# Attention output and second-parity x turned in 32x32 blocks by VectorE and put together through a DRAM scratch

## The chip, the cores and the metric

The kernel runs on one core of one Trainium2 chip. A core has a matrix engine (TensorE, PE in the profile), a vector engine (VectorE, DVE), a scalar engine (ScalarE, ACT), GpSimd (POOL) and SyncE (SP), which here only issues transfers to the core's 16 DMA engines. Each engine runs its own instructions in the order of the program and waits on semaphores for the others. The metric is the device time of one execution in microseconds (us). Lower is better.

## The reference

```python
x = A_x                                    # 1 x 2048 x 576, float32
xn = _layernorm(x, axis=-1)                # (x - mean) / sqrt(var + 1e-5)
return x + _A_ref(xn, A_wqkv, A_wo) + _B_ref(xn, B_w1, B_w2)

# _A_ref: 32 heads of 18; each position attends to itself and 7 earlier ones, 2 apart
qkv = xn @ wqkv                            # 576 -> 3 x 576
logits = einsum("bhsd,bhswd->bhsw", q, kg) * 18 ** -0.5     # masked where idx < 0
o = einsum("bhsw,bhswd->bhsd", softmax(logits), vg)
return o @ wo                              # 576 -> 576

# _B_ref
return relu(xn @ w1) @ w2                  # 576 -> 4608 -> 576
```

All of it is float32. The kernel reaches that accuracy with matmuls of a rounded type (float32r): each operand is split into a rounded part and the rest, and the products that matter are added.

## The kernel before

**Tiles and phases.** The attention only joins positions of one parity, since it steps by 2. So the kernel runs two phases (`ph` 0 and 1), one for each parity, of 1024 positions: 8 tiles (`i`) of 128 rows by 576 columns, held in `X`. A tile must also be there turned (columns on the partitions) as the operand of matmuls. 576 columns are 4 full groups of 128 and one of 64; the fifth group holds the 64 twice, so that one of its halves can carry the rounded part and the other the rest. Two tiles make one `XT` block of 256 positions (4 blocks, `tb`), with 9 groups: 4 rounded, 1 mixed, 4 rests.

**The loop and its order.** A phase has 144 steps: 12 chunks of the 4608 hidden columns, in each chunk 4 blocks `tb`, in each 3 slices `f` of 128 columns. The loop at line 547 writes out each engine's program step by step. In a step `n` it gives out, in this order: `run_splits` (weights that came by DMA are split by ACT and VectorE, and further loads issued), `h_mm(n+2)` (14 matmuls, then ReLU on ACT at line 447 and the rest on VectorE at line 448), the `at` list of the step, `o_mm(n)` (12 matmuls; after the third slice VectorE adds to `X` at line 471), the `late` list of the step, and `run_bg` (attention work of VectorE, as much as the planner's account of time allows). There are two buffers for the result of `h_mm` (`ph`), and `o_mm` works on what `h_mm` gave two steps earlier. Within an engine nothing is reordered.

**Attention** is taken in 4 units of 8 heads: `qkv_tile` on TensorE, the products and sums on VectorE from the `bg` queue into `QO`.

**Output projection.** From step 123 of a phase on, `wo_a` (late list) turns tile `i` of `QO` by five TensorE transposes (`transpose_split`, lines 273 and 274) into PSUM, and ACT and VectorE split it into `oT`. In the next step `wo_b` (at list) multiplies by the split `wo` in 28 matmuls, VectorE adds the result to `X`, and `done` stores the tile once it has all its parts. One tile is taken each step.

**Second-parity x.** At the end of phase 0 (the last chunk starts at step `e` = 132) the x tiles of phase 1 are loaded, `stats` and `norm` make the normalized tile `xn`, and `make_xt` turns it by five TensorE transposes and splits it into `XT`. Tile `i` has its `z = e + 3 + 2i`: load at `z - 6`, statistics late at `z - 2`, norm late at `z - 1`, `make_xt` at `z + 1`. The first `h_mm` of phase 1 that needs the block of tiles 6 and 7 is that of step 151.

**Queues.** All loads and stores but the halo copies of k and v are issued by SP, in program order: weights (lines 157 to 162, 173, 190 to 193, 210 to 213), x (235), out (432). Weights are loaded three tasks ahead of their split.

Of the kernel before, what the change touches and what calls it, by code (L numbers as in the profile page):

```python
# [10 lines left out]
F32 = mybir.dt.float32  # L11
F32R = mybir.dt.float32r
AF = mybir.ActivationFunctionType
ALU = mybir.AluOpType
# [3 lines left out]
P = 128  # L18
# [9 lines left out]
EPS = 1e-5  # L28

UNIT0, UNIT_STEP, WO_AT = 7, 27, 8  # L30
HEADW = (-5, -2, -1, 0, 0, 1)

HEAD = (
# [22 lines left out]
def tile_body(ctx: ExitStack, tc: tile.TileContext, x, wqkv, wo, w1, w2, out):  # L56
    nc = tc.nc
    S, D = x.shape
# [5 lines left out]
    KT = 4  # L64
    DR = D - KT * P
    D2 = D // 2
# [4 lines left out]
    ctx.enter_context(tc.manual_schedule())  # L71
    pool = lambda name, bufs, **k: ctx.enter_context(tc.tile_pool(name=name, bufs=bufs, **k))
    consts = pool("consts", 1)
    xp = pool("xp", 12)
    xtp = pool("xtp", NTB)
    qop = pool("qop", 1)
    kp = pool("kp", 1)
# [7 lines left out]
    lgp = pool("lgp", 2)  # L85
    smp = pool("smp", 2)
    tmp = pool("tmp", 2)
    ps_o = pool("ps_o", 2, space=PSUM)
    ps_h = pool("ps_h", 2, space=PSUM)
    ps_m = pool("ps_m", 2, space=PSUM)  # L90

    f32 = lambda ap: ap.bitcast(F32)
# [18 lines left out]
    def mm(o, l, r, start, stop, n):  # L111
        nc.tensor.matmul(o, l, r, start=start, stop=stop)  # L112
        t["pe"] += n / 2400.0 + 0.002

    def dve(n):
        t["dve"] += (n + 130) / 960.0
# [109 lines left out]
            split_task(step, *one(kt))  # L226


    X, XT, XN, MR = {}, {}, {}, {}

    def load_x(ph, i, parts=1):
        X[ph, i] = xp.tile([P, D], F32, name="x")
# [18 lines left out]

    def norm(ph, i, act=False):
        nm, r = MR.pop((ph, i))
        xn = tmp.tile([P, 640], F32, name="xn")
        if act:
            nc.scalar.activation(xn[:, 0:D], X[ph, i], AF.Identity, bias=nm)  # L256
            nc.scalar.activation(xn[:, 0:D], xn[:, 0:D], AF.Copy, scale=r)  # L257
        else:
            nc.vector.tensor_scalar(xn[:, 0:D], X[ph, i], nm, r, op0=ALU.add, op1=ALU.mult)
            dve(600)  # L260
        nc.scalar.activation(xn[:, D:640], xn[:, KT * P : D], AF.Copy)
        XN[ph, i] = xn

    def transpose_split(src, last, hi, mix, lo, free=False):

        if free:
            pa, pb = (ps_o.tile([P, 2, 512], F32, name="po")[:, 0, :] for _ in range(2))
            pa, pb = pa.rearrange("p (k c) -> p k c", k=KT), pb[:, 0:P]
        else:
            pa = ps_m.tile([P, KT, P], F32, name="pm")  # L270
            pb = ps_m.tile([P, P], F32, name="pm")
        for k in range(KT):
            nc.tensor.transpose(pa[:, k, :], src[:, k * P : (k + 1) * P], ident)  # L273
        nc.tensor.transpose(pb, last, ident)  # L274
        t["pe"] += 5 * 0.06
        nc.scalar.activation(hi, pa, AF.Copy)  # L276
        nc.vector.tensor_tensor(lo, pa, f32(hi), op=ALU.subtract)
        nc.scalar.activation(mix, pb, AF.Copy)
        nc.vector.tensor_tensor(mix[DR:P], pb[DR:P], f32(mix[DR:P]), op=ALU.subtract)
        dve(512)  # L280
        dve(128)

    def make_xt(ph, i, free=False):
        tb, h = divmod(i, 2)
        if h == 0:
            XT[ph, tb] = xtp.tile([P, 9, TBN], F32R, name="xT")
        d = XT[ph, tb][:, :, h * P : (h + 1) * P]
        xn = XN.pop((ph, i))
        transpose_split(xn[:, 0:512], xn[:, 512:640], d[:, 0:4, :], d[:, 4, :], d[:, 5:9, :], free)


    TERMS = [(k, k) for k in range(KT)] + [(5 + k, k) for k in range(KT)] + [(4, 4)] + [(k, 5 + k) for k in range(5)]


    QO, KK, VV = {}, {}, {}
# [109 lines left out]
    OT = {}  # L405

    def wo_a(ph, i):
        assert (ph, i) in ready, (ph, i, len(bg))
        o = QO[ph][:, i, :]
        od = tmp.tile([P, 2, DR], F32, name="od")  # L410
        nc.scalar.activation(od, o[:, None, KT * P : D].to_broadcast([P, 2, DR]), AF.Copy)
        d = tmp.tile([P, 9, P], F32R, name="oT", bufs=1)
        transpose_split(o[:, 0:512], od.rearrange("p a b -> p (a b)"), d[:, 0:4, :], d[:, 4, :], d[:, 5:9, :])
        OT[ph, i] = d

    def wo_b(ph, i):
        d, w = OT.pop((ph, i)), WO[ph]
        po = [ps_m.tile([P, D2], F32, name="pm") for _ in range(2)]
        for j, (a, b) in enumerate(TERMS):
            for h in range(2):  # L420
                mm(po[h], d[:, a, :], w[b][:, h * D2 : (h + 1) * D2], j == 0, j == len(TERMS) - 1, D2)
        for h in range(2):
            acc = X[ph, i][:, h * D2 : (h + 1) * D2]
            nc.vector.tensor_tensor(acc, po[h], acc, op=ALU.add)
            dve(D2)
# [53 lines left out]
    def at(n, f, *a):  # L479
        todo.setdefault(n, []).append((f, a))  # L480
# [3 lines left out]
    def late(n, f, *a):  # L484
        todo_late.setdefault(n, []).append((f, a))

    plan = []
    for ph in range(NPH):
        b = ph * SPP
        for c in range(NCH):  # L490
            for f in range(C):
                s = b + c * SPC + f
                first = ph == c == 0
                plan.append((HEADW[f] if first else s - 5, w1_task, ((ph, c, f), c * C + f)))
                plan.append((HEADW[3 + f] if first else s - 3, w2_task, ((ph, c, f), c * C + f)))
        for u in range(NU):
            s = b + UNIT0 + u * UNIT_STEP
            plan.append((s - 5, wq_tasks, ((ph, u), u)))
            for i in range(NI):
                at(s + i, qkv_tile, ph, u, i)  # L500
            late(s + NI + 1, attention, ph, u)
        s = b + UNIT0 + NU * UNIT_STEP + WO_AT
        plan.append((s - 8, wo_tasks, (ph,)))
        for i in range(NI):
            late(s + i, wo_a, ph, i)
            at(s + i + 1, wo_b, ph, i)
            at(s + i + 1, done, ph, i)
        if ph + 1 < NPH:
            e = b + SPP - SPC
            for i in range(NI):  # L510
                z = e + 3 + 2 * i
                at(z - 6, load_x, ph + 1, i)
                late(z - 2, stats, ph + 1, i)
                late(z - 1, norm, ph + 1, i)
                at(z + 1, make_xt, ph + 1, i)
    for step, f, a in sorted(plan, key=lambda z: z[0]):
        if f in (wq_tasks, wo_tasks):
            f([step + k for k in range(5)], *a)
# [13 lines left out]
    held = []  # L532
    run_splits(-5)
    norm(0, 0)
    norm(0, 1)
    stats(0, 2)
    make_xt(0, 0)
    make_xt(0, 1, True)
    for f in held:
        f()  # L540
# [45 lines left out]
```

## Time and profile before

| | |
|---|---|
| median of 3 runs | 1194.38 us (1193.45 to 1194.89) |
| the profiled execution | 1194.74 us, span 1193.0 us |
| granted TensorE clock, mean | 0.998 |
| DMA | 75.67 MB, mean 63 GB/s |
| transposes of x in phase 1 (L273, L274) | 8 tiles, 580.3 to 629.0 us |
| transposes of the attention output | 16 tiles, 504.3 to 564 and 1092 to 1147 us |

The page's first part gives each engine's busy time and its share of the span; PEld is the loading of weights into TensorE, which overlaps the matmuls. A row of the order of time has the start in us, the duration in us, the engine, the line of the kernel, the operation, the tiles (out<-in) with the shape, the number of instructions merged into the row, and in brackets how long the engine had been idle and what ended that. A row of the groups has the number of instructions, the busy time in us, the mean duration in ns, and the idle time before them. A row of the stretches has for each engine the busy time and the number of instructions, then the granted clock, the share of time in which the DMA engines were busy, and GB/s.

### The profile page before, as it was taken

What the parts mean: (1) busy time and instruction counts of PE and PEld (TensorE: products, weight loads), DVE (VectorE), ACT (ScalarE), POOL (GpSimd) and SP (SyncE); (2) the same over time, 40 slices, a digit from 0 to 9 for tenths busy, and PEclk for the clock granted to TensorE, in tenths of its full rate; (3) what the DMA queues carried; (4) which work ended last, traced back from release to release, by engine and by line L of the source; (5) the groups of instructions that cost most, each with busy time, mean ns of one, the idle gap of its engine ahead of it and who ended that gap; (6) DMA issues with size and microseconds to landing.
All of it is one profiled execution on the core that took longest, in us unless ns stands there. A gap on an engine that the chain in (4) does not pass through costs nothing.

```text
span 1193.0 us, 21739 instructions
## 1 busy us (share of the span) xinstructions
PE 1183.8 (99%) x9016; PEld 1172.8 (98%) x9016; DVE 812.5 (68%) x1269; ACT 310.5 (26%) x790; POOL 40.1 (3%) x63
## 2 busy tenths in 40 slices
PE   8999999999999999999999999999999999999998
PEld 7999999999999999999999999999999999999998
DVE  7516875888687578875573278858767875886732
ACT  5422222131222222322233123122221322222210
POOL 2000000010000000000120000000100000000000
PEclk9999999999999999999999999999999999999999
DMA  5312122130321311402242113031302312212002
GB/s 172 84 32 82 42 76 55 38 107 1 98 58 44 86 33 43 114 11 73 91 130 74 46 54 90 22 85 29 86 21 79 83 38 79 63 42 73 21 1 80
DMA packets 84883, 75.67 MB, mean 63 GB/s; under 512 B 6592, under 2 KB 68288, under 8 KB 84784
## 3 DMA queue, kind: packets, MB, share of 16 engines
q1 hardware_dynamic: 82256, 66.08, 19.7%
q10 hardware_dynamic: 2528, 8.20, 2.4%
q8 instruction: 71, 1.16, 0.4%
q14 instruction: 28, 0.23, 0.1%
HBM read 61.34 MB, written 4.72 MB: 55 GB/s over the span
## 4 chain that ended last, share of the span: by engine, by line
PE 98%; DVE 1%; SPq 0%; ACT 0%; DMA 0%; issue 0%; DVEq 0%; ACTq 0%
PE ph L112 39%; PE po L112 38%; PE pm L112 20%; PE pm L273 1%; PE pm L274 0%; DMA st<-in_w 0%; SPq L235 0%; DVE pr L380 0%; DVE pr L373 0%; SPq L157 0%; SPq L162 0%; SPq L161 0%; PE po L273 0%; ACT xn L257 0%; ACT xn L256 0%
## 5 line engine op out<-in xcount | busy, mean ns | idle before, releaser
L112 PE MATMUL ph<-xT,w1t 128*128 128x256 f32 x4032 | 514.2, 279 | 1.3 <-ACT xT L276 0.6
L112 PEld LDWEIGHTS ph<-xT,w1t 128*128 128x128 f32 x4032 | 491.6, 188 | 2.0 <-ACT xT L276 0.8
L112 PE MATMUL po<-w2t,hhi 128*128 128x288 f32 x2304 | 400.5, 296 | 0.4 <-DVE w2t L143 0.3
L112 PEld LDWEIGHTS po<-w2t,hhi 128*128 128x128 f32 x2304 | 337.0, 188 | 2.0 <-DVE w2t L143 0.5
L447 ACT ACTIVATE hhi<-ph 128x256 fp32r<-128x256 f32 x288 | 110.2, 382 | 531.8 <-PE ph L112 512.5
L112 PE MATMUL po<-w2t,hlo 128*128 128x288 f32 x1152 | 244.7, 293 | 0.0
L448 DVE SCALAR_TENSOR_TENSOR hlo<-ph,hhi 128x256 fp32r<-128x256 f32 x288 | 121.7, 423 | 169.1 <-ACT hhi L447 167.8
L471 DVE TENSOR_TENSOR x<-po,x 128x576 f32<-128x576 f32 x192 | 143.9, 757 | 69.8 <-PE po L112 66.3
L112 PE MATMUL pm<-wq,xT 128*128 128x432 f32 x896 | 185.5, 358 | 0.0
L112 PEld LDWEIGHTS po<-w2t,hlo 128*128 128x128 f32 x1152 | 183.7, 188 | 0.0
L112 PEld LDWEIGHTS pm<-wq,xT 128*128 128x128 f32 x896 | 163.8, 188 | 5.6
L343 DVE TENSOR_TENSOR pr<-qo,k 128x1152 f32<-128x1152 f32 x64 | 85.9, 1349 | 0.0
L373 DVE TENSOR_TENSOR pr<-lg,v 128x1152 f32<-128x1152 f32 x64 | 85.0, 1352 | 0.3
L346 DVE TENSOR_REDUCE lg<-pr 128x64 f32<-128x1152 f32 x64 | 85.0, 1343 | 0.0
L143 DVE TENSOR_TENSOR w2t<-st,w2t 128x576 fp32r<-128x576 f32 x72 | 54.3, 755 | 45.0 <-ACT w2t L146 44.7
L380 DVE TENSOR_TENSOR pr<-pr 128x288 f32<-128x288 f32 (+1 forms) x128 | 70.5, 602 | 0.1
L143 DVE TENSOR_TENSOR w1t<-st,w1t 128x640 fp32r<-128x640 f32 x72 | 59.0, 820 | 15.0 <-ACT w1t L146 14.8
L146 ACT ACTIVATE w2t<-st 128x576 fp32r<-128x576 f32 x72 | 49.1, 684 | 45.0 <-PE po L112 31.0
L146 ACT ACTIVATE w1t<-st 128x640 fp32r<-128x640 f32 x72 | 53.0, 737 | 13.2 <-DMA st<-in_w 13.2
L312 ACT ACTIVATE k<-pm 128x144 f32<-128x144 f32 x64 | 18.7, 292 | 142.8 <-PE pm L112 142.6
L112 PE MATMUL pm<-wq,oT 128*128 128x288 f32 x352 | 51.7, 299 | 0.0
L112 PEld LDWEIGHTS pm<-wq,oT 128*128 128x128 f32 x352 | 47.9, 188 | 1.7
(63 smaller groups left out, 398.0 us busy)
## 6 DMA issues: line engine op xcount, KB each, us to landing
st<-in_w SPq DMA_DIRECT2D x72, 288.0 KB, 3.0
st<-in_w SPq DMA_DIRECT2D x72, 256.0 KB, 3.0
st<-in_wqkv SPq DMA_DIRECT2D x32, 216.0 KB, 3.0
st<-in_w SPq DMA_DIRECT2D x144, 32.0 KB, 2.7
out<-x SPq DMA_DIRECT2D x16, 288.0 KB, 2.1
x<-in_x SPq DMA_DIRECT2D x15, 288.0 KB, 3.9
k<-k ACTq DMA_DIRECT2D x8, 441.0 KB, 3.9
v<-v ACTq DMA_DIRECT2D x8, 441.0 KB, 4.6
```

Of the source, the lines that this page charges most:

```text
L112: nc.tensor.matmul(o, l, r, start=start, stop=stop)
L143: nc.vector.tensor_tensor(lo, src, f32(hi), op=ALU.subtract)
L146: nc.scalar.activation(hi, src, AF.Copy)
L273: nc.tensor.transpose(pa[:, k, :], src[:, k * P : (k + 1) * P], ident)
L312: nc.scalar.activation(k[:, W - 1 + i, :], pq[:, 1, :], AF.Copy)
L343: nc.vector.tensor_tensor(pr[i], q, window(k, i), op=ALU.mult)
L346: nc.vector.tensor_reduce(lg[:, i], pr.pop(i).rearrange(heads, d=Dh), axis=AX.X, op=ALU.add)
L373: nc.vector.tensor_tensor(pr[i].rearrange(heads, d=Dh), e, window(v, i).rearrange(heads, d=Dh), op=ALU.mult)
L380: nc.vector.tensor_tensor(o, z[:, 0:n], z[:, n : 2 * n], op=ALU.add)
L447: nc.scalar.activation(hi, pt, AF.Relu)
L448: nc.vector.scalar_tensor_tensor(lo, pt, 0.0, f32(hi), op0=ALU.max, op1=ALU.subtract)
L471: nc.vector.tensor_tensor(acc, PO[k][:, :, 0:D2], acc, op=ALU.add)
```

## The change

Three things change.

1. **How a tile is turned.** A new `turn` lets VectorE transpose the 576 columns in 32x32 blocks (and the last 64 columns a second time, which fills the fifth group). Each of four transfers then takes one quarter of the partitions (32 rows) to a DRAM scratch `turned`, block by block, in runs of 32 values, so that the scratch holds the whole turned tile. `fetch` is the fifth transfer, back into SBUF in runs of 128 values. All five are issued by SP; the fetch waits for the four writes. `split` is what followed the TensorE transposes, now reading SBUF.
2. **Where it is used.** For the attention output of both phases and for x of phase 1. The x of phase 0 is still turned by TensorE (`transpose_split`).
3. **The schedule.** The output projection takes tiles at the steps 0, 1, 3, 4, 6, 7, 9, 10 from its start: turn late in step z, fetch in z + 1, split late in z + 2, `wo_b` in z + 3. The x tiles have `z = e + 2 + 2i`. For tiles 0 and 1 loading, statistics and norm stay spread over steps; for tiles 2 to 7 the load is in z - 2, and statistics, norm and turn are all late in z. The fetch is in z + 1 and `make_xt` late in z + 2, which is the step z of the next tile, where it stands first in the list. The pool of x tiles has 10 buffers in place of 12, `xn` three in place of two (the fetched attention output uses them too, and the rests are written over it), `oT` five groups in place of nine.

```diff
+WO_STEPS = (0, 1, 3, 4, 6, 7, 9, 10)
...
-    xp = pool("xp", 12)
+    xp = pool("xp", 10)
...
+    turned = pool("turned", 3, space=bass.MemoryType.DRAM)
...
-        xn = tmp.tile([P, 640], F32, name="xn")
+        xn = tmp.tile([P, 640], F32, name="xn", bufs=3)
...
-        nc.scalar.activation(xn[:, D:640], xn[:, KT * P : D], AF.Copy)
+        if ph == 0:
+            nc.scalar.activation(xn[:, D:640], xn[:, KT * P : D], AF.Copy)
...
+    def turn(src, key):
+        tr = tmp.tile([P, 5, P], F32, name="tr")
+        flat = tr.rearrange("p k c -> p (k c)")
+        nc.vector.transpose(flat[:, 0:D], src)
+        nc.vector.transpose(flat[:, D:640], src[:, KT * P : D])
+        dve(D)
+        dve(DR)
+        TD[key] = turned.tile([5 * 4, 32, P], F32, name="turned")
+        for r in range(4):
+            rows = slice(32 * r, 32 * r + 32)
+            nc.sync.dma_start(
+                TD[key][:, :, rows].rearrange("g j i -> j g i"),
+                flat[rows, :].rearrange("j (g i) -> j g i", i=32),
+            )
+
+    def fetch(dst, key):
+        nc.sync.dma_start(dst, TD.pop(key).rearrange("(k c) j i -> (c j) k i", k=5))
+
+    def turn_x(ph, i):
+        turn(XN[ph, i][:, 0:D], (ph, i))
+
+    def fetch_x(ph, i):
+        fetch(XN[ph, i].rearrange("p (k c) -> p k c", c=P), (ph, i))
+
+    def split(z, hi, mix, lo):
+        nc.scalar.activation(hi, z[:, 0:KT], AF.Copy)
+        nc.scalar.activation(mix, z[:, KT], AF.Copy)
+        nc.vector.tensor_tensor(lo, z[:, 0:KT], f32(hi), op=ALU.subtract)
+        nc.vector.tensor_tensor(mix[DR:P], z[DR:P, KT], f32(mix[DR:P]), op=ALU.subtract)
+        dve(512)
+        dve(128)
...
+        if ph:
+            split(xn.rearrange("p (k c) -> p k c", c=P), d[:, 0:4, :], d[:, 4, :], d[:, 5:9, :])
+            return
...
-        o = QO[ph][:, i, :]
-        od = tmp.tile([P, 2, DR], F32, name="od")
-        nc.scalar.activation(od, o[:, None, KT * P : D].to_broadcast([P, 2, DR]), AF.Copy)
-        d = tmp.tile([P, 9, P], F32R, name="oT", bufs=1)
-        transpose_split(o[:, 0:512], od.rearrange("p a b -> p (a b)"), d[:, 0:4, :], d[:, 4, :], d[:, 5:9, :])
-        OT[ph, i] = d
+        turn(QO[ph][:, i, :], (ph, i))
+
+    def wo_f(ph, i):
+        OT[ph, i] = tmp.tile([P, 5, P], F32R, name="xn", bufs=3)
+        fetch(f32(OT[ph, i]), (ph, i))
+
+    def wo_s(ph, i):
+        z = OT[ph, i]
+        d = tmp.tile([P, 5, P], F32R, name="oT", bufs=1)
+        split(f32(z), d[:, 0:4], d[:, 4], z[:, 0:4])
+        OT[ph, i] = [d[:, k] for k in range(5)] + [z[:, k] for k in range(4)]
...
         for i in range(NI):
-            late(s + i, wo_a, ph, i)
-            at(s + i + 1, wo_b, ph, i)
-            at(s + i + 1, done, ph, i)
+            z = s + WO_STEPS[i]
+            late(z, wo_a, ph, i)
+            at(z + 1, wo_f, ph, i)
+            late(z + 2, wo_s, ph, i)
+            at(z + 3, wo_b, ph, i)
+            at(z + 3, done, ph, i)
         if ph + 1 < NPH:
             e = b + SPP - SPC
             for i in range(NI):
-                z = e + 3 + 2 * i
-                at(z - 6, load_x, ph + 1, i)
-                late(z - 2, stats, ph + 1, i)
-                late(z - 1, norm, ph + 1, i)
-                at(z + 1, make_xt, ph + 1, i)
+                z = e + 2 + 2 * i
+                at(z - 2 if i > 1 else z - 6, load_x, ph + 1, i)
+                late(z - 2 if i < 2 else z, stats, ph + 1, i)
+                late(z - 1 if i < 2 else z, norm, ph + 1, i)
+                late(z if i < 2 else z, turn_x, ph + 1, i)
+                at(z + 1, fetch_x, ph + 1, i)
+                late(z + 2, make_xt, ph + 1, i)
```

More of the change, by code (lines that the diff above doesn't have):

```diff
@@ L226, in wo_tasks @@
             split_task(step, *one(kt))
-    X, XT, XN, MR = {}, {}, {}, {}
+    X, XT, XN, MR, TD = {}, {}, {}, {}, {}
     def load_x(ph, i, parts=1):
@@ L420, in wo_b @@
             for h in range(2):
-                mm(po[h], d[:, a, :], w[b][:, h * D2 : (h + 1) * D2], j == 0, j == len(TERMS) - 1, D2)
+                mm(po[h], d[a], w[b][:, h * D2 : (h + 1) * D2], j == 0, j == len(TERMS) - 1, D2)
         for h in range(2):
```

## The prediction

> **What bounds the kernel now.** I read the page first: shares of busy time, then the chain of work that ended last.
>
> ```profile
> PE 1183.8 (99%) x9016; PEld 1172.8 (98%) x9016; DVE 812.5 (68%) x1269; ACT 310.5 (26%) x790; POOL 40.1 (3%) x63
> PE 98%; DVE 1%; SPq 0%; ACT 0%; DMA 0%; issue 0%; DVEq 0%; ACTq 0%
> ```
>
> TensorE is the chain almost from end to end, so work taken off it is time gained, and any new wait of it is time lost. Next the order of time in the two stages that the change touches. First the end of phase 0, where x of the second parity is turned: a plain step, then one with five transposes.
>
> ```profile
> 588.99 1.78 PE L112 MATMUL ph<-xT,w1t 128*128 128x256 f32 x14
> 590.60 0.69 PE L112 MATMUL po<-w2t,hhi 128*128 128x288 f32 x4
> 592.19 1.78 PE L112 MATMUL ph<-xT,w1t 128*128 128x256 f32 x14
> 593.81 0.60 PE L273 MATMUL pm<-ident,xn 128*128 128x128 f32 x4
> 594.44 0.60 ACT L276 ACTIVATE xT<-pm 128x512 fp32r<-128x512 f32 x1
> 595.07 0.69 DVE L277 TENSOR_TENSOR xT<-pm,xT 128x512 fp32r<-128x512 f32 x1 [0.17 <-ACT xT L276]
> 595.80 0.29 DVE L279 TENSOR_TENSOR xT<-pm,xT 64x128 fp32r<-64x128 f32 x1
> 595.94 1.78 PE L112 MATMUL ph<-xT,w1t 128*128 128x256 f32 x14
> 630.71 1.78 PE L112 MATMUL ph<-xT,w1t 128*128 128x256 f32 x14
> ```
>
> A plain step takes 592.19 - 588.99 = 3.20 us (1.61 for h_mm, 1.59 for o_mm); with five transposes 595.94 - 592.19 = 3.75, so a turn costs TensorE 0.55. The split after it takes 594.44 to 596.09, 1.65 us over ACT and VectorE. The last row is h_mm of step 151, the first that needs all of tiles 6 and 7.
>
> Then the output projection, at its first tile (step 123 and 124).
>
> ```profile
> 501.18 1.78 PE L112 MATMUL ph<-xT,w1t 128*128 128x256 f32 x14
> 503.75 0.42 DVE L448 SCALAR_TENSOR_TENSOR hlo<-ph,hhi 128x256 fp32r<-128x256 f32 x1
> 504.84 1.85 PE L112 MATMUL ph<-xT,w1t 128*128 128x256 f32 x14
> 506.53 3.24 PE L112 MATMUL pm<-wq,oT 128*128 128x288 f32 x22
> 510.40 0.69 PE L112 MATMUL po<-w2t,hhi 128*128 128x288 f32 x4
> 512.45 1.85 PE L112 MATMUL ph<-xT,w1t 128*128 128x256 f32 x14
> ```
>
> wo_b is 510.40 - 506.53 = 3.87 us; the whole step of 512.45 - 504.84 = 7.61 is 3.20 + 3.87 + 0.54, so the turn costs the same here.
>
> **What is removed.** 16 attention tiles and 8 x tiles: 24 x 0.55 = 13.2 us of TensorE, all on its chain. That is the most that the change can give. The small ACT copies that fed the fifth transpose go too; ACT is 26% busy, so that is worth nothing.
>
> **What is added, beside other work.** Two VectorE transposes a tile. No row shows one. The nearest rows are VectorE passes over 576 and few columns:
>
> ```profile
> L259 DVE TENSOR_SCALAR xn<-x,nm,rstd 128x576 f32<-128x576 f32 x11 | 6.9, 626 | 0.8 <-POOL rstd L248 0.7
> L143 DVE TENSOR_TENSOR w2t<-st,w2t 128x576 fp32r<-128x576 f32 x72 | 54.3, 755 | 45.0 <-ACT w2t L146 44.7
> L244 DVE BATCH_NORM_AGGREGATE mv<-bst 128x2 f32<-128x12 f32 x16 | 3.3, 209 | 0.6
> ```
>
> I take 0.9 us for the pair (bounds 0.8, and 1.8 for half speed). 24 x 0.9 = 22 us on an engine that is idle a third of the span costs nothing as occupation. It counts as latency.
>
> **What is added as latency: W, the time from the turn to the last landing of its four writes.** Each write is 640 packets of 128 B, so a tile puts 4 x 640 / 16 = 160 on each of 16 DMA engines; the fetch is 640 packets of 512 B, 40 on each. No data packet below 512 B is in the trace. Prices come from two stretches with loads alone, of 512 B packets and of 2304 B rows:
>
> ```profile
> DMA packets 1376, 0.66 MB, mean 109 GB/s; under 512 B 96, under 2 KB 1376, under 8 KB 1376
> q1 hardware_dynamic: 1376, 0.66, 39.5%
> ...
> DMA packets 432, 0.88 MB, mean 140 GB/s; under 512 B 48, under 2 KB 48, under 8 KB 432
> q1 hardware_dynamic: 432, 0.88, 46.3%
> ...
> st<-in_w SPq DMA_DIRECT2D x72, 256.0 KB, 3.0
> out<-x SPq DMA_DIRECT2D x16, 288.0 KB, 2.1
> ...
> 644.22 0.38 SPq L157 DMA_DIRECT2D st<-in_w  x1
> 644.65 0.51 SPq L161 DMA_DIRECT2D st<-in_w  x1
> 645.21 0.59 SPq L162 DMA_DIRECT2D st<-in_w  x1
> ```
>
> The first stretch is 6.0 us: 0.395 x 6.0 x 16 = 37.9 engine-us over 1280 data packets (96 are completions), 29.6 ns each. The second is 6.3 us: 46.7 over 384, 122 ns each. A line through the two gives 9.9 ns at 128 B: the lower end. The upper end is two 512 B packets, 59 ns, if each small write is a read and a write. I take 29.6, the price of the smallest packet that the trace shows, since nothing in it shows that cutting a packet below 512 B makes it cheaper. The fixed part of a transfer: 3.0 us to landing, less 32 packets x 29.6 ns = 0.95, leaves 2.05. So W = 2.05 + 160 x 0.0296 = 6.8 us. The fetch F = 2.05 + 40 x 0.0296 = 3.2. With the lower price SP's issue decides (0.43 to 0.56 us from one to the next): W = 3 x 0.5 + 2.05 + 0.4 = 4.0. With the upper, W = 2.05 + 9.5 = 11.5.
>
> By the Trainium skill, "VectorE: DVE Perf Modes", section "The three transpose paths", a plain strided copy takes 19 times the 1309 ns of the crossbar for 128x128 bf16; spread as 1024 two-byte packets on each engine that is 24 ns a packet, an estimate that would make W 5.9 and the time about 1245. No run here shows it.
>
> **The x stage, where most is lost.** The schedule puts, in the late list of one step, make_xt(i), then stats(i+1), norm(i+1), turn_x(i+1), for i from 1. Engines run in program order. ACT and VectorE stop in make_xt(i) until its fetch has landed, and the statistics of the next tile are queued behind that. So the tiles don't overlap: one loop is split, statistics and norm, turn, W, F. Statistics to norm, without a pause of the program, at the start of the kernel:
>
> ```profile
> 5.13 0.82 DVE L243 BATCH_NORM_STATS2 bst<-x 128x6 f32<-128x288 f32 x2 [0.86 <-DMA x<-in_x]
> 6.47 0.84 POOL L248 TENSOR_TENSOR rstd<-mv,mhalf 128x1 f32<-128x1 f32 x1
> 7.34 0.58 DVE L259 TENSOR_SCALAR xn<-x,nm,rstd 128x576 f32<-128x576 f32 x1 [0.47 <-POOL rstd L248]
> ```
>
> That is 7.92 - 5.13 = 2.79. The loop L = 1.65 + 2.79 + 0.9 + 6.8 + 3.2 = 15.3 us, and two steps of TensorE are 6.4. TensorE runs on for about two steps past a held ACT, since ph has two buffers and o_mm lags by two; then it waits for ReLU, which is queued behind the split. SP's queue is in the same order: behind the fetch's wait stand the next x load, the out stores and the weight loads, none needed within the wait.
>
> When does it end? From 501.18 with plain steps of 3.20, wo_b 3.87 in steps 126, 127, 129, 130, 132, 133, 135, 136 and no transposes, h_mm(127) starts at 517.85, h_mm(134) at 559.6, h_mm(136) at 569.9 and h_mm(151) would start at 621.7. Split 7 of the output projection must end by its wo_b, 569.9 + 1.7 = 571.6, so its fetch is issued by 566.75, and then x's first writes: 567.2 + 6.8 + 3.2 + 1.65 = 578.9 for split 0; tile 1 follows at 578.9 + 0.9 + 6.8 + 3.2 + 1.65 = 591.4; six loops more, 6 x 15.3 = 92: 683.4. Against 630.71 h_mm(151) is 52.7 us late, the transposes' gain so far already in it.
>
> **The output projection.** For the first tile the turn ends at 504.2 + 0.9 = 505.1 (VectorE is free at 504.17), the split at 505.1 + 6.8 + 3.2 + 1.65 = 516.75; wo_b(0) could start at 512.4: 4.35 us. SP issues the writes of a pair's second tile only behind the wait of the first one's fetch, and split(2k+1) precedes turn(2k+2): a pair's loop is 0.9 + 6.8 + 0.5 + 6.8 + 3.2 + 1.65 = 19.85, against 3 x 3.20 + 2 x 3.87 = 17.34 of TensorE, 2.5 us more, three times. With 0.2 at the second tile: 4.35 + 0.2 + 7.5 = 12.05 a phase.
>
> **Sum.** Phase 0 and the x stage 52.7 + 12.05 = 64.8; phase 1 has 8 transposes less, -4.4, and 12.05 more. Together +72.4. The profiled execution took 1194.74 us, its span 1193.0; the 1.7 outside stays. The median of the runs is 1194.38, within 0.4 of it. 1194.7 + 72.4 = 1267.
>
> **Rivals.**
> (a) Small packets are cheap (9.9 ns) and W = 4.0. L is 12.5, the pair 14.25, which TensorE covers. Split 1 is then in time, at 584.3, and h_mm(151) at 584.3 + 75 = 659.3, 28.6 late; the first wo tile 1.55 twice, -4.4: +27.3, 1222. For it: the line through two sizes. Against: it reaches below both.
> (b) A write below 512 B costs a read and a write, 59 ns, W = 11.5. L = 20.0; the pair 29.25, 11.9 over, three times, and 9.05 + 4.9 before: 49.7 a phase. Split 1 at 600.8, h_mm(151) at 720.8: 90 + 99.4 - 4.4 = +185, 1380. For it: twice the packet price of the trace; against it: no row of this kernel shows such a write. The Trainium skill, "DMA: Bandwidth & Descriptors", section "Specifications", has this rule: under 512 B the DMA reads, changes and writes; no run here shows it so far.
> (c) Faster: the loop isn't closed, statistics of the next tile run while ACT waits, and each tile has only its own delay. It decides if VectorE reaches stats(i+1) before fetch(i) lands. Then 13.2 is gained, with W = 4.0 1.55 is lost at each first wo tile, and the last tile, turned in step 148 (612.1 + 2.4 + 12.5 = 627.0 against 621.7), costs 5.3 at most: 1194.7 - 13.2 + 3.1 + 0 to 5.3 = 1185 to 1190. Against: the order of the late list, and L at its least (2.1 for the writes' landing) is still above 6.4.
> (d) The clock. After waits at the start of the kernel it fell:
>
> ```profile
> 10.00:15.00 5.00, 4.49 (x24) 4.20 (x24) 3.70 (x8) 3.06 (x6) 0.00 (x0) 0.66 0.99 341
> ```
>
> At 0.66, two steps are 9.7 us, below any L here, so waits in the x stage hide it; behind the last one it adds 2 to 3 us. It is within the range, no case of its own.
>
> **How the numbers follow.** Forecast (W from 5.5 to 8) 0.48, (a) 0.32, (b) 0.14, (c) 0.06. The likeliest gives 1267. The range goes from a little below (a), 1216, to 1335 (W near 9.5), and leaves out (b) and (c). What can be told from no change is 0.2%, 2.4 us: slower 0.94, within 0.01, faster 0.05.
>
> **What would show it.** No transposes on TensorE after the head of the kernel. TensorE idle in waits of some 9 us, once every two steps, from about step 138 to 151, ended by ACT's ReLU or by xT; before those, ACT idle for the DMA into xn. The four writes landing 6 to 7 us after the turn and the fetch 3.2 after. TensorE waiting for oT at the first wo_b of each phase by about 4 us. I am wrong if those waits are absent, if VectorE's statistics run ahead of the split before them, or if W is outside 4 to 11.5.

## The result and the profile after

The changed kernel takes 1223.19 us (median, 1222.41 to 1223.52) where the kernel before takes 1194.64 beside it: a ratio of 1.024, 95% interval 1.0225 to 1.0256. It is slower by 28.5 us; the forecast was slower by 72. The profiled execution took 1223.48 us with a span of 1221.7.

The page after: busy shares, the chain that ended last, the new issues of transfers (tiles, engine, count, KB each, median us to landing).

```profile
PE 1178.7 (96%) x8896; PEld 1167.4 (96%) x8896; DVE 827.9 (68%) x1317; ACT 306.5 (25%) x766; POOL 38.9 (3%) x63
PE 90%; DMA 4%; DVE 3%; SPq 1%; issue 1%; ACT 1%; POOL 0%; DVEq 0%; POOLq 0%; ACTq 0%
...
turned<-tr SPq DMA_DIRECT2D x96, 80.0 KB, 2.1
xn<-turned SPq DMA_DIRECT2D x24, 320.0 KB, 3.2
```

TensorE has 120 instructions less and is no longer the whole chain: transfers hold 4% of it, VectorE 3%. Next, for whom TensorE waited (us in total, times, longest), first in the output projection and then in the x stage of the changed kernel:

```profile
PE pm L114 <- ACT oT L295: 0.3, 1, 0.3
...
PE po L114 <- DVE x L517: 16.4, 2, 10.5
PE ph L114 <- DVE hlo L494: 9.6, 4, 6.4
PE ph L114 <- ACT xT L295: 7.3, 2, 3.8
```

The first row is all of phase 0's output projection: 0.3 us. The others, 33.3 us, lie between 580 and 680 us. They name VectorE's sum and rest (L517, L494) and ACT's rounded part of xT (L295), but those engines weren't busy: in their programs these instructions stood behind a split of xT that waited for its fetch. In order of time, one loop of that stage, from one split of xT to the next (a selection of the rows):

```profile
609.72 0.63 ACT L295 ACTIVATE xT<-xn 128x512 fp32r<-128x512 f32 x1 [9.42 <-DMA xn<-turned]
611.39 0.82 DVE L245 BATCH_NORM_STATS2 bst<-x 128x6 f32<-128x288 f32 x2
613.40 0.58 DVE L261 TENSOR_SCALAR xn<-x,nm,rstd 128x576 f32<-128x576 f32 x1 [0.76 <-POOL rstd L250]
614.02 0.78 DVE L272 STREAM_TRANSPOSE tr<-xn 128x576 f32<-128x576 f32 x1
614.95 2.05 SPq L279 DMA_DIRECT2D turned<-tr  x4
616.70 1.30 PE L114 MATMUL po<-w2t,hhi 128*128 128x288 f32 x4 [5.84 <-DVE x L517]
618.53 0.38 SPq L285 DMA_DIRECT2D xn<-turned  x1
622.52 0.63 ACT L295 ACTIVATE xT<-xn 128x512 fp32r<-128x512 f32 x1 [10.86 <-DMA xn<-turned]
```

ACT was idle for 9.4 and 10.9 us for the transfer into xn, and the next tile's statistics begin the moment the split is through (611.39). The steps of the loop: split 1.67, statistics and norm 2.6, turn 0.9, the four writes 618.53 - 614.95 = 3.58, the fetch 3.99: 12.8 us for two steps of TensorE that take 6.4. In the turns of tiles 1 to 7 the writes take 3.6 to 5.5 us by the same two rows, 4.0 in the mean; the three longer ones (4.1 to 5.5) have two or three weight loads issued between the last write and the fetch. From the first to the last of six loops (splits at 584.60 and 662.36):

```profile
584.60 0.63 ACT L295 ACTIVATE xT<-xn 128x512 fp32r<-128x512 f32 x1 [3.14 <-DMA xn<-turned]
662.36 0.63 ACT L295 ACTIVATE xT<-xn 128x512 fp32r<-128x512 f32 x1 [11.43 <-DMA xn<-turned]
663.04 3.19 PE L114 MATMUL ph<-xT,w1t 128*128 128x256 f32 x14 [3.80 <-ACT xT L295]
670.40 1.77 PE L114 MATMUL ph<-xT,w1t 128*128 128x256 f32 x14
```

A loop is 77.76 / 6 = 12.96 us in the mean. h_mm(151) starts at 663.04 in place of 630.71, 32.3 us late, and runs at a lowered clock (3.19 us for what takes 1.78; by the microsecond the granted clock was 0.50 from 663 to 665 and 1.00 from 666 on). The granted clock by longer stretches (columns as before; the third figure from the end is the clock):

```profile
615.00:630.00 15.00, 12.33 (x80) 12.13 (x81) 8.47 (x19) 1.94 (x5) 0.75 (x2) 0.78 0.52 132
645.00:660.00 15.00, 3.72 (x17) 3.24 (x16) 7.23 (x15) 2.28 (x6) 2.81 (x4) 0.66 0.37 89
```

Last, the output projection. A step with wo_b, and the wo_b in it, in the changed kernel:

```profile
518.12 1.76 PE L114 MATMUL ph<-xT,w1t 128*128 128x256 f32 x14
519.73 1.22 PE L114 MATMUL pm<-wq,oT 128*128 128x288 f32 x8
523.44 0.69 PE L114 MATMUL po<-w2t,hhi 128*128 128x288 f32 x4
525.03 1.77 PE L114 MATMUL ph<-xT,w1t 128*128 128x256 f32 x14
```

The step takes 6.91 us in place of 7.61; wo_b itself 523.44 - 519.73 = 3.71 in place of 3.87. So a turned tile of the attention output gives 0.70 us, more than the transposes' 0.54.

### The profile page after: what moved, and what is told of

Same layout as the page of the kernel before. It is cut to its first block, busy times and chain, and to the rows that moved or that the text cites. A ratio compares the mean times of both kernels' runs of the same rounds, so it can differ in the third digit from the quotient of the medians.

```text
span 1221.7 us, 21744 instructions
## 1 busy us (share of the span) xinstructions
PE 1178.7 (96%) x8896; PEld 1167.4 (96%) x8896; DVE 827.9 (68%) x1317; ACT 306.5 (25%) x766; POOL 38.9 (3%) x63
## 4 chain that ended last, share of the span: by engine, by line
PE 90%; DMA 4%; DVE 3%; SPq 1%; issue 1%; ACT 1%; POOL 0%; DVEq 0%; POOLq 0%; ACTq 0%
PE ph L114 35%; PE po L114 35%; PE pm L114 19%; DMA xn<-turned 2%; DMA turned<-tr 1%; SPq L279 1%; DMA x<-in_x 1%; DVE bst L245 1%; DVE xn L261 0%; POOL rstd L250 0%; DVE pr L421 0%; ACT xT L295 0%; DVE xT L297 0%; DVE x L517 0%; DVE mv L246 0%
## 5 line engine op out<-in xcount | busy, mean ns | idle before, releaser
L114 PEld LDWEIGHTS ph<-xT,w1t 128*128 128x128 f32 x4032 | 495.9, 190 | 21.4 <-DVE hlo L494 10.5
L114 PE MATMUL po<-w2t,hhi 128*128 128x288 f32 x2304 | 402.6, 297 | 17.5 <-DVE x L517 16.4
L494 DVE SCALAR_TENSOR_TENSOR hlo<-ph,hhi 128x256 fp32r<-128x256 f32 x288 | 121.0, 420 | 161.6 <-ACT hhi L493 160.8
L517 DVE TENSOR_TENSOR x<-po,x 128x576 f32<-128x576 f32 x192 | 143.4, 756 | 69.9 <-PE po L114 67.1
L145 DVE TENSOR_TENSOR w1t<-st,w1t 128x640 fp32r<-128x640 f32 x72 | 58.7, 817 | 12.6 <-ACT w1t L148 12.5
L148 ACT ACTIVATE w1t<-st 128x640 fp32r<-128x640 f32 x72 | 52.9, 735 | 11.0 <-DMA st<-in_w 10.9
L390 POOL TENSOR_SCALAR_AFFINE_SELECT lg<-lg 1x512 f32<-1x512 f32 x8 | 9.4, 1172 | 848.6 <-DVE lg L387 848.6
L114 PE MATMUL pm<-wq,oT 128*128 128x288 f32 x224 | 35.2, 296 | 0.6 <-ACT oT L295 0.6
```

What stands on the lines that cost most here:

```text
L145: nc.vector.tensor_tensor(lo, src, f32(hi), op=ALU.subtract)
L148: nc.scalar.activation(hi, src, AF.Copy)
L494: nc.vector.scalar_tensor_tensor(lo, pt, 0.0, f32(hi), op0=ALU.max, op1=ALU.subtract)
L517: nc.vector.tensor_tensor(acc, PO[k][:, :, 0:D2], acc, op=ALU.add)
```

## The experiments

Two theories stood against each other. The first: the order of the late list closes a loop over each x tile, so that split, statistics, norm, turn, writes and fetch stand one behind the other. The second: the transfers themselves, their packets or SP's queue, are too slow for any order. And within the loop it was open what makes up the time of the four writes.

**One use at a time.** First x back on TensorE, the attention output as changed (the pool of 10 x buffers stays, so loads come two steps later than before):

```diff
...
-                z = e + 2 + 2 * i
-                at(z - 2 if i > 1 else z - 6, load_x, ph + 1, i)
...
+                z = e + 3 + 2 * i
+                at(z - 6 if i < 2 else z - 4, load_x, ph + 1, i)
+                late(z - 2, stats, ph + 1, i)
+                late(z - 1, norm, ph + 1, i)
+                at(z + 1, make_xt, ph + 1, i)      # transpose_split again
```

> The attention output is turned by VectorE and DRAM as in the change; x of the second parity by TensorE again, its loads two steps later than before (10 buffers). If the loss lies in the x stage alone: 16 turns of 0.55 us are gained, less some 0.7 us of waits at the first tile of each phase, so 1186 to 1187.5 us, and no wait of TensorE over 1 us between 560 and 640 us. If the turns of the attention output cost time as well (the fuller forecast had 12 us of waits a phase): 1195 us or more.

Measured: 1184.1 us, 0.9908 of the kernel before (0.9893 to 0.9923), faster than both kernels. TensorE's only wait between 480 and 680 us is this one:

```profile
PE pm L310 <- DVE x L466: 0.4, 1, 0.4
```

So all of the loss lies in the x stage. The gain is larger than the transposes: 16 x 0.70 = 11.2 us by the step shown above, 11.4 measured (1195.47 for the kernel before beside it). The expectation, with 0.55 a turn, was 2 us too high.

Then the complement, the attention output back on TensorE and x as changed:

```diff
-            z = s + WO_STEPS[i]
-            late(z, wo_a, ph, i)
...
+            late(s + i, wo_a, ph, i)               # transpose_split again, 9 groups in oT
+            at(s + i + 1, wo_b, ph, i)
```

> The complement: the attention output by TensorE as before, x of the second parity by VectorE and DRAM as in the change. If the loss is the closed loop of the x stage alone: the changed kernel's 1223.2 plus the 16 x 0.55 = 8.8 us that the attention output gave, 1229 to 1233 us, with steps of about 12.6 us from one split of xT to the next. If the two uses disturb each other on SP's queue, this one loses less: under 1225 us.

Measured: 1240.42 us, 1.0378 (1.036 to 1.0395), above the expected range. This kernel also has one buffer in place of two for the turned blocks `tr` and for `od`. The two uses don't disturb each other on SP's queue; together they lose less. The last split of xT:

```profile
673.25 0.63 ACT L295 ACTIVATE xT<-xn 128x512 fp32r<-128x512 f32 x1 [11.00 <-DMA xn<-turned]
```

It is at 673.25, against 662.36 in the changed kernel, so 10.9 of the 17.2 us between the two arise by then, and 8 x 0.70 = 5.6 in phase 1. The 10.9 are there before the loop starts: the turn of x tile 0 starts at 576.66 in place of 564.15 and split 1 at 596.04 in place of 584.60, and the six loops from there take 77.2 us in place of 77.8. Of it 8 x 0.70 = 5.6 is the gain that is missing. The other 5 fit the schedule: in the changed kernel two wo_b (steps 135 and 136, 7.4 us) fall behind the first turn of x and so within its latency, here all are over by then. That is read from the steps and the trace; no run tried it.

**The loop opened.** One line moved: in a step's late list make_xt(i) stands behind the turn of tile i + 1.

```diff
-                late(z + 2, make_xt, ph + 1, i)
+            for i in range(NI):
+                late(e + 4 + 2 * i, make_xt, ph + 1, i)
```

> The changed kernel with one line moved: in a step's late list make_xt(i) stands behind statistics, norm and turn of tile i+1, not ahead of them. If the closed loop (the next tile's statistics queued behind the wait for this tile's fetch) is the cause, two tiles are in flight, the splits come about 6.5 to 7.5 us apart in place of 12.6, and the time is 1182 to 1195 us. If the latency of turn, writes and fetch itself is the cause, whatever the order, ACT is still held for each tile and the time stays above 1208 us.

Measured: 1197.1 us, 1.0018 (1.0006 to 1.003). 26 of the 28.5 us are gone, though 2 us more were left than the range allowed. The splits are now 8.4 us apart (601.55 to 635.09, four intervals), in place of 12.96 but wider than the 6.5 to 7.5 that were expected:

```profile
601.55 0.63 ACT L295 ACTIVATE xT<-xn 128x512 fp32r<-128x512 f32 x1 [5.50 <-DMA xn<-turned]
605.92 0.81 DVE L245 BATCH_NORM_STATS2 bst<-x 128x6 f32<-128x288 f32 x2
608.53 0.78 DVE L272 STREAM_TRANSPOSE tr<-xn 128x576 f32<-128x576 f32 x1
608.82 0.63 ACT L295 ACTIVATE xT<-xn 128x512 fp32r<-128x512 f32 x1 [5.33 <-DMA xn<-turned]
...
635.09 0.63 ACT L295 ACTIVATE xT<-xn 128x512 fp32r<-128x512 f32 x1 [5.14 <-DMA xn<-turned]
```

The statistics (605.92) and turn (608.53) of the next tile now come ahead of the split (608.82). ACT still waits 2 to 5.5 us for each fetch, and its ReLUs wait with it. Against x on TensorE (1184.1 us) this order is still 13 us slower, so the order of the list is the larger part of the x stage's loss and not all of it.

**A part taken out of the loop.** Statistics and norm of tiles 2 to 7 one step earlier, so that they don't stand behind the split; the turn still does.

```diff
-                at(z - 2 if i > 1 else z - 6, load_x, ph + 1, i)
-                late(z - 2 if i < 2 else z, stats, ph + 1, i)
-                late(z - 1 if i < 2 else z, norm, ph + 1, i)
...
+                at(z - 3 if i > 1 else z - 6, load_x, ph + 1, i)
+                late(z - 2 if i < 2 else z - 1, stats, ph + 1, i)
+                late(z - 1, norm, ph + 1, i)
```

> The changed kernel with statistics and norm of x tiles 2 to 7 one step earlier (late in z - 1, load in z - 3), so that they no longer stand behind the split of the tile before; the turn still does. If the loop is split, statistics and norm, turn, writes, fetch, the statistics and norm (2.8 us) drop out of it: the splits of xT come 9.5 to 10.5 us apart in place of 12.96, six loops save 15 to 20 us, and the time is 1203 to 1209 us. If the loop isn't closed over them (the time of the transfers on SP's queue alone sets the pace), the spacing stays above 12 us and the time above 1218.

Measured: 1205.47 us, 1.0089 (1.0071 to 1.0107), in the middle of the range. The loop:

```profile
603.45 0.63 ACT L295 ACTIVATE xT<-xn 128x512 fp32r<-128x512 f32 x1 [7.27 <-DMA xn<-turned]
605.12 0.78 DVE L272 STREAM_TRANSPOSE tr<-xn 128x576 f32<-128x576 f32 x1
606.05 2.05 SPq L279 DMA_DIRECT2D turned<-tr  x4
608.25 0.81 DVE L245 BATCH_NORM_STATS2 bst<-x 128x6 f32<-128x288 f32 x2
609.63 0.38 SPq L285 DMA_DIRECT2D xn<-turned  x1
613.65 0.63 ACT L295 ACTIVATE xT<-xn 128x512 fp32r<-128x512 f32 x1 [8.26 <-DMA xn<-turned]
```

The turn follows the split at once and the statistics run while the writes are under way: 613.65 - 603.45 = 10.2 us. Writes (3.58) and fetch (4.0) are as before. So the loop is what the sum says it is (12.8 less the 2.6 of statistics and norm), and its parts add.

**Turned further ahead.** make_xt three steps after the turn, and the tiles' steps closer together at the end.

```diff
-                z = e + 2 + 2 * i
+                z = e + (2, 4, 6, 8, 9, 11, 13, 15)[i]
...
-                late(z + 2, make_xt, ph + 1, i)
+            for i in range(NI):
+                late(e + (2, 4, 6, 8, 9, 11, 13, 15)[i] + 3, make_xt, ph + 1, i)
```

> The changed kernel with make_xt three steps after the turn in place of two, behind the turns of the same step, and the tiles' steps z at 2, 4, 6, 8, 9, 11, 13, 15 from step 132. If latency is all that is left once the loop is open (turn 6 us after the step's start, landing 7 us later, 13.2 against 9.6 + 2 of cover for ACT and two more steps for TensorE), the waits of TensorE in the x stage fall under 6 us and the time is 1178 to 1188 us, at or below the kernel with x on TensorE. If the engines' order still closes a loop over two tiles, the splits stay over 8 us apart and the time is 1192 us or more.

Measured: 1193.87 us, 0.9998 (0.9984 to 1.0013), so the rival's side; the splits of tiles 1 to 7 (584.52 to 632.85, six intervals) are 8.1 us apart, which is the rival's sign too, if barely. TensorE's waits from 570 to 640 us still add up to 10.7 us. SP's queue shows a possible reason:

```profile
598.59 0.39 SPq L285 DMA_DIRECT2D xn<-turned  x1
599.03 0.52 SPq L237 DMA_DIRECT2D x<-in_x  x1
599.59 3.63 SPq L279 DMA_DIRECT2D turned<-tr  x4
603.32 0.57 SPq L192 DMA_DIRECT2D st<-in_wqkv  x1
606.24 0.38 SPq L285 DMA_DIRECT2D xn<-turned  x1
```

A turn ready at 598.3 gets its first write out at 599.59, behind another tile's fetch and an x load; its own four take 3.63 in place of 2.05, and its fetch goes out 6.65 us after the first write in place of 3.58. So with two tiles in flight the order of SP's queue lengthens a tile's way. Whether that sets the pace, or the order of ACT and VectorE still does, wasn't separated.

**What makes up the time of the writes.** Three kernels write the same bytes with other packets or in another number of transfers. In all three the scratch has another order and the fetch reads it as plain rows, still in runs of 128 values, so what reaches the matmuls is not the turned tile. First one transfer, with the same packets of 128 B:

```diff
...
-        for r in range(4):
-            rows = slice(32 * r, 32 * r + 32)
-            nc.sync.dma_start(
-                TD[key][:, :, rows].rearrange("g j i -> j g i"),
-                flat[rows, :].rearrange("j (g i) -> j g i", i=32),
-            )
+        nc.sync.dma_start(
+            TD[key].rearrange("(g a) (b i) -> (a b) g i", g=20, i=32),
+            flat.rearrange("p (g i) -> p g i", i=32),
+        )
```

> The four writes of a turn become one transfer with the same 2560 packets of 128 B; the scratch then has another order and the fetch reads it in plain rows, so the operands of the matmuls are not the turned tiles. If the price is per issue and a fixed time to landing (packets near nothing), the time from the first issue to the fetch's issue falls from 3.9 to about 2.2 us, the loop to about 10.9, and the kernel to about 1210 us. If a packet costs the 9.9 ns of the line through two sizes, 160 on an engine take 1.6 us: 3.6 us, and the time hardly moves (1219 to 1223). At 29.6 ns it would be 6.8 us and over 1240.

Then one transfer of whole rows, `TD[key].rearrange("(p k) i -> p (k i)", k=5)` from `flat`:

> One write of 128 rows of 2560 B in place of four of 128 B packets (the scratch isn't the turned tile, so the matmul operands differ). 8 packets of about 135 ns on an engine: with 2.05 fixed some 2.1 to 3.1 us from issue to the fetch's issue, whatever a small packet costs; the kernel 1208 to 1217 us.

And four transfers of 32 whole rows each:

> Four writes as in the change, each of 32 rows of 2560 B (the scratch isn't the turned tile, so the matmul operands differ). If the issue of four transfers by SP sets the time, it stays at 3.7 to 4.0 us from the first issue to the fetch's issue, and the kernel stays at 1221 to 1224 us. If the small packets set it, it falls by at least 1 us and the kernel by 8 us or more.

SP's rows of the three, in this order: first write (with the number merged) and the fetch that waits for it.

```profile
614.10 0.37 SPq L277 DMA_DIRECT2D turned<-tr  x1
617.47 0.37 SPq L283 DMA_DIRECT2D xn<-turned  x1
```

```profile
610.69 0.32 SPq L277 DMA_DIRECT2D turned<-tr  x1
612.89 0.37 SPq L280 DMA_DIRECT2D xn<-turned  x1
```

```profile
612.73 1.71 SPq L279 DMA_DIRECT2D turned<-tr  x4
615.82 0.38 SPq L282 DMA_DIRECT2D xn<-turned  x1
```

| writes | first issue to fetch | time |
|---|---|---|
| 4 x 640 packets of 128 B (the change) | 3.58 us | 1223.2 us |
| 1 x 2560 packets of 128 B | 3.37 us | 1218.8 us |
| 4 x 32 rows of 2560 B | 3.09 us | 1218.2 us |
| 1 x 128 rows of 2560 B | 2.20 us | 1213.1 us |

Small packets alone cost 1.2 us (3.37 against 2.20), four issues alone 0.9 (3.09), both together 1.4 (3.58). That is less than the sum of the two, as it would be if packets of one transfer move while the next is issued. Neither of the two plain answers (the issue alone, the packets alone) holds. The table's times are from one turn each, among the shortest of its kernel. Over the seven turns of tiles 1 to 7 the means are 4.0, 3.4, 3.4 and 2.3 us, in the order of the table, and seven times their differences from the change, 4.3, 4.7 and 12.3 us, come near what the kernels gained: 4.4, 5.0 and 10.1. Each of the three kernels ran once.

## Why the prediction was right and wrong

**Right: the mechanism and its place.** The closed loop of the x stage was forecast from the order of the late list, with its parts, and is shown by three things: the loop read from the trace, the line moved (26 us back), and the statistics taken out of it (18 us back, as worked out). Split 1.65 (1.67 measured), statistics and norm 2.79 (2.6) and turn 0.9 (0.9: the two transposes run 0.77 and 0.20) were well sized. The fetch, 3.2, took 3 to 4 us.

**Wrong: W, the time of the four writes.** The prediction priced a 128 B packet at 29.6 ns, like one of 512 B, and gave W = 6.8 us; measured, about 3.6 in four of the seven turns of tiles 1 to 7, 4.0 in their mean, and 5.5 at most, with weight loads between. Two terms in it were too large. The packet: in the changed kernel the stretch with one turn's writes alone (504.80 to 508.80 us) shows

```profile
DMA packets 2624, 0.33 MB, mean 82 GB/s; under 512 B 2624, under 2 KB 2624, under 8 KB 2624
q1 hardware_dynamic: 2624, 0.33, 47.1%
```

0.471 x 4.0 x 16 = 30.1 engine-us over 2560 data packets, 11.8 ns each: close to the line through the two sizes (9.9), far from 29.6. And the fixed part: 2.05 us was taken from loads. The stores' own row was quoted beside it and not used: 288 KB in 2.1 us, of which 8 packets on an engine at 122 ns are 0.98, leaves 1.1. The one transfer of whole rows fits that: 2.20 us, of which 8 packets of some 135 ns (an estimate, from the line through the two sizes) are 1.1. With 1.1 and 160 x 11.8 ns = 1.9 the writes would take 3.0 us. Of the 0.6 that is missing, four issues in place of one are 0.2 (3.58 against 3.37); what makes up the other 0.4 stays open.

**What followed from W.** In the x stage six loops of 15.3 became 12.96: 14 us. Split 1 ended earlier, at 586.3 in place of 591.4: 5 us. In the output projection a pair's loop is 6.25 + 2 x 3.6 = 13.4 us, with the longest writes 6.25 + 2 x 5.5 = 17.25, and no longer above TensorE's 17.34, so the 12.05 us of waits a phase became 0.3 and 0.4: 23.4 us. Of the 72.4 that leaves 30; measured, 28.5. The smaller rest is of both signs: h_mm(151) started at 663.04, 1.0 ahead of the end of the last split (664.04), where the prediction let it wait for that end; in phase 1 wo_b gives 8 x 0.16 = 1.3 us that nothing in the prediction saw (phase 0's part is in the time of split 1 already); the lowered clock takes 1.4 (step 151 takes 670.40 - 663.04 = 7.36, the next of its kind 5.92).

**The signs.** The waits of some 9 us, once every two steps, came as eight waits of up to 10.5 us, 33.3 in all. Half of that (16.4) was ended by VectorE's sum into `X`, which the prediction hadn't named beside ReLU and xT; it stood behind the same split. The wait for oT at the first wo_b of a phase was 0.3 and 0.4 us in place of about 4. And W, at its shortest 3.58, lies below the 4 that the prediction named as a sign of being wrong.

**The rivals.** (a), small packets cheap, gave 1222 and came within 1.2 us: its W of 4.0, its loop of 12.5, its h_mm(151) at 659.3 (663.0). Part of that closeness is luck: its six loops are 2.8 us too short, and its two waits of 1.55 at the first wo tiles are 2.4 too long. Its split 1 at 584.3 isn't worked out; with the forecast's terms and W = 4.0 it would end at 585.8 (586.3 measured). What it rested on stood in the prediction: two packet sizes lay on a line with 3.3 ns at zero bytes. That no row showed a small packet to be cheaper was no reason to price it like a large one. (b), 59 ns for a write below 512 B, is refuted: such a write is 11.8 ns. The Trainium skill, "DMA: Bandwidth & Descriptors", section "Specifications", has read, change and write below 512 B; if it takes place, these runs show no such price. The 24 ns a packet that the prediction estimated from the Trainium skill, "VectorE: DVE Perf Modes", section "The three transpose paths", are twice what was measured. (c), the loop not closed, fell: the statistics never ran ahead of the split. (d), the clock, was as described: down to 0.66 over a stretch, hidden in the waits, and 1.4 us behind the last one, where 2 to 3 were forecast.

## What to carry to other kernels

Where an engine runs in the order of the program, a wait put ahead of the next item's first work turns a latency into a loop; moving one line, so that work that waits for nothing stands ahead of the wait, gave back 26 of 28.5 us here. A turn through VectorE and DRAM has some 8.5 us of latency from the transposes to the fetched tile and takes 0.55 to 0.70 us off TensorE: it paid for the attention output, where a schedule with three steps between covers it (1184.1 us against 1195.5 for the kernel before), and for the x tiles in none of the orders tried. Price a small transfer from stores if it is a store, and with a line through packet sizes, before taking the price of the next larger packet.

## What the runs showed of the hardware

A DRAM write in packets of 128 B took 11.8 ns of an engine for each packet, where packets of 512 B (loads) took 29.6. That is 2 ns above the line through the two larger sizes and 1.6 times as much for each byte; the price of a read and a write, 59 ns, does not show. VectorE's 32x32 transposes of 576 float32 columns took 0.77 us, like a pass of `tensor_tensor` over them (0.755). Without the transposes ahead of it wo_b took 3.71 us in place of 3.87, for the same 28 matmuls; the cause wasn't looked for and stays open.
